# First batch element with all of V in fp32, low parts of the second over ScalarE and GpSimd, and a new program order for both

## The chip, the cores and the metric

The kernel runs on one core of one Trainium2 chip. The metric is device time in microseconds (us) of one execution. The engines are TensorE (PE, its weight loads PEld), VectorE (DVE), ScalarE (ACT), GpSimd (POOL) and SyncE (SP, which here only issues DMAs). Each runs its own instructions strictly in the order in which the program lists them and waits on semaphores for the others.

## The reference, cut to what matters

```python
# x: (8, 8, 512, 64), state: (8, 8, 32, 64)
xread = softmax(x @ state.T / 8) @ state        # 512 tokens per batch element and head
sread = softmax(state @ x.T / 8) @ x            # 32 slots per batch element and head
x = concat([xread, sread], axis=2)              # -> 8*544 tokens, 512 features
h = x @ w_in                                    # w_in: 512 x 2048
g = where(h >= 1, h, where(h <= -1, 0, (h + 1)**2 / 4))
x = g @ w_out                                   # w_out: 2048 x 512
...
logits = x @ phi                                # soft MoE: 32 slots, softmax over tokens and over slots
out = c @ (relu(slot_input @ w1) @ w2)          # 8 experts
```

## The kernel before, in words

The 8 batch elements are called b = 0 to 7; a ninth pass (b = 8) takes the state tokens. For one b, `attention(b)` makes the attention weights a (two halves G, each 128 x 512), and `vchunk(b, c)` multiplies the state with a quarter c of `w_in`, which gives V (two halves of 128 x 512 in PSUM). `hstep(b, m)`, m = 0 to 15, then makes a block h of 128 x 512 of the hidden layer as V times a, since xread @ w_in = a @ (state @ w_in); chunk c serves m = 4c to 4c+3.

fp32 products are made exact enough in one of two ways. In the *split* form each operand is written as a high part in fp32r (ACT copies it) and a low part in fp32r (the operand less its high part, a subtraction), and h is the sum of six fp32r matmuls: per half G high by high, high by low and low by high (line 478). In the *plain* form h is the sum of two fp32 matmuls (line 469). Before, only chunk 0 of b = 0 is plain. Every other chunk of V has two low parts, made by DVE at line 428 (`v<-V,v`), or, for the entries of the table `lP` and 2 <= b < 7, by an extra ACT copy `Vs` and a GpSimd subtraction (line 426).

The activation takes h to g: ACT makes c = relu(h/2 + 1/2) out of PSUM, GpSimd squares it (line 508), DVE makes g = min(max(h, 1), c) (line 532). Three PSUM banks hold h (`psH`), so the h of m + 3 needs the g of m. DVE then transposes g into `gp` (line 552, `tstep`); four transposes belong to four m. `estep` multiplies four g with the product of w_out and phi, `smblock(b)` updates the running softmax and `fall` accumulates.

`w_in` and `w_out` come as 64 bit numbers. They are loaded in 16 pieces of 1 MB into six staging buffers, and `words(i, ...)` turns piece i into fp32: ACT copies two bytes per number into a rim (two instructions, 128x1024 bytes each), and DVE makes two passes (lines 169 and 171). For the pieces in `dv`, DVE makes three passes alone (lines 156, 158, 160). Pieces 0 to 7 are `w_in` (chunk c needs 2c and 2c+1), 8 to 15 are `w_out`; of the latter each pair is multiplied with phi (`wps`) and written back to DRAM. The conversions of pieces 2 to 15 lie between the hsteps of b = 0, as do the steps of `attention(1)`.

From b = 2 on, `steady` sets an order on PE that is written by hand and repeats for each b. For b = 0 and b = 1 the main loop sets it (`V0`, `Vn`: at which m a chunk's V is made; `E0`, `T0`: estep and transposes of b = 0; `attA`: steps of attention(2) in b = 1), and a scheduler orders each engine's list from that program order and the dependencies.

PSUM for V (`psV`) is one tile of two banks. The attention scores S of b = 1 and 2 lie in the same tile.

Of the kernel before, what the change touches and what calls it, by code (L numbers as in the profile page):

```python
# [17 lines left out]


@with_exitstack  # L20
def kernel(
# [14 lines left out]
    nc = tc.nc  # L36
# [180 lines left out]
    def attention(b):  # L217
# [180 lines left out]
    v0t = []

    def vlate(b):  # L400
        if not v0t:
            v0t.append(slot("v0", dt=F32R))
        return hilo(v0t[0])
# [473 lines left out]
    A = None  # L877
    for b in range(B + 1):
        last = b == B
        if 2 <= b < B:  # L880
# [9 lines left out]
            run["s_gc"] = slot("s_gc", tag="v1")  # L890
        for m in range(NM):
            if b == 0:
                for _ in range(CFG["todo"][m]):
                    todo.pop(0)()
            if last and m == 0:
                give("a1")
# [42 lines left out]
            if b == 1:
# [187 lines left out]
```

## Time and profile before

| | |
|---|---|
| Time, median of 3 runs | 508.49 us (507.92 to 510.24) |
| The profiled execution | 508.4 us |
| Its span, first to last instruction | 506.6 us |
| PE, DVE, ACT, POOL busy | 89%, 73%, 53%, 46% of the span |
| Mean granted clock of TensorE | 0.958 of full speed |

The span has three stages: loads, conversions and b = 0 (to about 93 us), b = 1 to 7 (41.7 us for each in the steady part), and the ninth pass with the experts. An average over the span says little on the first stage, so the rows further down are taken stretch by stretch.

### The profile page before, as it was taken

The page shows a single profiled execution, that of the slowest core. Times are in us where ns is not written, and L with a number is a line of the kernel's source. Part 1 is how long each engine was busy: PE and PEld are TensorE (multiplying, and loading weights), DVE is VectorE, ACT ScalarE, POOL GpSimd, SP SyncE. Part 2 cuts the span into 40 slices and gives each one's busy share as a digit, 9 for nine tenths or more (in the row PEclk, how much of TensorE's full clock was granted, in tenths as well). Part 3 has the DMA queues.
Part 4 walks back from the last instruction along what each step waited for, and adds up shares of the span by engine and source line. Part 5 has one row for each costly group of instructions (what it writes and reads, how often), then busy time and mean ns, then how long its engine had stood idle before and what let it go on. Part 6 is the DMA issues. An engine that isn't in the chain of part 4 may idle for free.

```text
span 506.6 us, 11018 instructions
## 1 busy us (share of the span) xinstructions
PE 451.7 (89%) x4497; PEld 262.5 (52%) x4497; DVE 371.1 (73%) x670; ACT 269.9 (53%) x485; POOL 234.6 (46%) x224
## 2 busy tenths in 40 slices
PE   5397859989999999999999999999989999897881
PEld 3133424545555565546555565556647798533450
DVE  2878997997797797699779779778788785340341
ACT  2899667463673674476367367455445476210331
POOL 2344533563873785586488379465442100020320
PEclk9679978999999999999999999999999999997995
DMA  8999756600310220220040031033054597799699
GB/s 311 419 421 416 232 208 216 242 1 3 96 72 1 84 85 1 84 85 0 3 167 2 2 98 71 1 98 153 2 208 144 193 403 292 286 425 413 238 307 293
DMA packets 22689, 85.83 MB, mean 169 GB/s; under 512 B 2032, under 2 KB 10608, under 8 KB 14576
## 3 DMA queue, kind: packets, MB, share of 16 engines
q1 hardware_dynamic: 22128, 84.62, 44.8%
q8 instruction: 35, 0.57, 0.5%
q0 software_dynamic: 512, 0.53, 0.5%
q14 instruction: 14, 0.11, 0.1%
HBM read 72.03 MB, written 13.11 MB: 168 GB/s over the span
## 4 chain that ended last, share of the span: by engine, by line
PE 51%; DVE 26%; DMA 10%; ACT 5%; POOL 3%; issue 2%; SPq 0%; DVEq 0%; ACTq 0%; POOLq 0%
PE h L478 19%; DMA w<-in_w_dram 6%; DVE gp L552 5%; DVE g L532 5%; PE h L486 4%; PE E L118 4%; PE FV L124 3%; PE V L118 3%; DMA gp<-in_win_dram 3%; PE FX L124 2%; PE SO L1034 2%; DVE wD L171 2%; DVE z L281 2%; PE wtp L783 2%; POOL a L316 2%
## 5 line engine op out<-in xcount | busy, mean ns | idle before, releaser
L478 PE MATMUL h<-a,v 128*128 128x512 f32 x744 | 198.4, 410 | 10.8 <-DVE g L532 5.2
L508 POOL TENSOR_TENSOR c<-c 128x512 f32<-128x512 f32 x128 | 136.2, 1071 | 127.1 <-ACT c L129 117.9
L478 PEld LDWEIGHTS h<-a,v 128*128 128x128 f32 x744 | 133.2, 190 | 83.9 <-issue 29.5
L129 ACT ACTIVATE c<-h,half 128x512 f32<-128x512 f32 x128 | 87.9, 690 | 102.6 <-PE h L478 79.9
L532 DVE SCALAR_TENSOR_TENSOR g<-h,c 128x512 f32<-128x512 f32 x112 | 75.7, 676 | 20.9 <-POOL c L508 20.7
L552 DVE STREAM_TRANSPOSE gp<-g 128x512 f32<-128x512 f32 x112 | 78.9, 705 | 2.3
L129 ACT ACTIVATE v<-V 128x512 fp32r<-128x512 f32 x62 | 37.4, 603 | 12.7 <-PE V L124 7.8
L118 PE MATMUL V<-win,st_t 64*32 64x512 f32 x64 | 34.4, 618 | 2.8 <-ACT att L129 2.8
L124 PE MATMUL V<-win,st_t 64*32 64x512 f32 x448 | 36.7, 618 | 0.0
L124 PE MATMUL FX<-gp,dR 32*32 32x512 f32 x512 | 35.6, 598 | 0.0
L124 PE MATMUL FV<-gp,dR 32*32 32x512 f32 x496 | 35.4, 597 | 0.0
L118 PE MATMUL E<-g,wp 128*32 128x512 f32 x56 | 29.2, 604 | 1.8 <-DVE g L532 1.4
L428 DVE TENSOR_TENSOR v<-V,v 128x512 fp32r<-128x512 f32 x42 | 28.3, 674 | 2.7 <-ACT v L129 2.2
L124 PE MATMUL E<-g,wp 128*32 128x512 f32 x168 | 29.6, 605 | 0.0
L284 POOL TENSOR_TENSOR att<-att,z 128x512 f32<-128x512 f32 x16 | 18.1, 1136 | 24.1 <-DVE rz L246 16.8
L426 POOL TENSOR_TENSOR v<-Vs,v 128x512 fp32r<-128x512 f32 x20 | 25.9, 1294 | 5.1 <-ACT Vs L129 5.1
L486 PE MATMUL h<-XSh,v 128*128 128x256 f32 x128 | 25.0, 287 | 0.0
L661 DVE SCALAR_TENSOR_TENSOR acc<-acc,al,FV 128x256 f32<-128x256 f32 (+1 forms) x20 | 10.6, 584 | 18.1 <-PE FX L124 18.1
L1069 DVE COPY o<-oV 128x512 f32<-128x512 f32 x6 | 4.2, 692 | 25.6 <-PE oX L124 25.6
L1077 POOL DMA_DIRECT2D out_dram<-o x16 | 8.0, 509 | 30.4 <-DVE o L1069 30.4
L486 PEld LDWEIGHTS h<-XSh,v 128*128 128x128 f32 x128 | 20.2, 188 | 1.2 <-issue 0.8
L271 PE MATMUL eTp<-cst_t,att 128*128 128x128 f32 x64 | 11.3, 305 | 10.2 <-ACT att L129 10.1
(242 smaller groups left out, 779.5 us busy)
## 6 DMA issues: line engine op xcount, KB each, us to landing
w<-in_w_dram SPq DMA_DIRECT2D x22, 1024.0 KB, 9.6
xn<-in_xn_dram SPq DMA_DIRECT2D x8, 1024.0 KB, 4.9
out_dram<-o SPq DMA_DIRECT2D x16, 512.0 KB, 5.5
xs<-in_xs_dram SPq DMA_DIRECT2D x7, 1024.0 KB, 4.8
gp<-in_w_dram SPq DMA_DIRECT2D x6, 1024.0 KB, 7.6
gp<-in_wout_dram SPq DMA_DIRECT2D x5, 1024.0 KB, 10.4
wb<-in_win_dram SPq DMA_DIRECT2D x4, 1024.0 KB, 12.3
wo<-wD SPq DMA_DIRECT2D x16, 256.0 KB, 3.3
```

What stands on the lines that cost most here:

```text
L118: first = mm(**calls[0])
L124: e = mm(**c)
L129: return nc.scalar.activation(out=out, in_=in_, func=func, **kw)
L271: nc.tensor.transpose(p[:, st, :], e2[G][:, 128 * st:128 * st + 128], ident)
L284: (nc.vector if b in CFG["mulD"] else nc.gpsimd).tensor_tensor(out=t3, in0=t3, in1=z1.unsqueeze(2).to_broadcast([128, 16, 32]), op=ALU.mult)
L426: nc.gpsimd.tensor_tensor(out=lo[:, G, :], in0=Vs, in1=hi[:, G, :], op=ALU.subtract)
L428: nc.vector.tensor_tensor(out=lo[:, G, :], in0=V[G], in1=hi[:, G, :], op=ALU.subtract)
L478: mm(out=h, lhsT=v[:, G, f], rhs=a[:, G, :], start=(k == 0), stop=(k == 5))
L486: mm(out=h, lhsT=w[:, j, :], rhs=x[:, j, :], start=(k == 0), stop=(k == 11))
L508: nc.gpsimd.tensor_tensor(out=c, in0=c, in1=c, op=ALU.mult)
L532: gI[b, m] = nc.vector.scalar_tensor_tensor(out=g, in0=h, scalar=1.0, in1=c, op0=ALU.max, op1=ALU.min)
L552: nc.vector.transpose(out=gd_of(b, m), in_=gT[b, m])
```

## The change

Four edits to code and a set of tables:

- `f32` lists the chunks of b = 0 that are plain: now 0, 1, 2 and 3. Their V goes out of PSUM in two ACT copies, with no low parts; a of b = 0 is used as it is, so its high parts (two ACT copies) and low parts (two GpSimd subtractions, line 316) are gone. All 16 hsteps of b = 0 are two fp32 matmuls.
- `lP1` sends six of the eight low parts of b = 1 over the ACT copy `Vs` and GpSimd: all but (chunk 0, G 0) and (chunk 3, G 1). (`lP0` has no effect, since no chunk of b = 0 is split.)
- `gv0` and `gv1` let ACT square c, instead of GpSimd, for m = 3, 5, 11 of b = 0 and m = 4, 6 of b = 1.
- Order: chunks 1, 2, 3 of b = 0 at m = 2, 4, 6 (were 2, 6, 10) and of b = 1 at m = 1, 4, 8 (were 0, 4, 10); the conversions at other m (`cpos`); pieces 7 and 9 on DVE alone (were 10 and 12); the steps of attention(1) and attention(2), the esteps and transposes of b = 0 at other m; 10 warming matmuls instead of 14.

```diff
-CFG = dict(..., dv=(10,12), V0=(2, 6, 10), Vn=(0, 4, 10), ..., warm=14, ...)
+CFG = {'cpos': (1, 1, 2, 4, 4, 5, 8, 9, 10, 11, 11, 11, 12, 13), ..., 'lP1': ((0, 1), (1, 0), (1, 1), (2, 0), (2, 1), (3, 0)), ..., 'f32': (0, 1, 2, 3), ...}
...
         def back():
+            araw[b] = raw
+            if b == 0 and 3 in CFG["f32"]:
+                for G in range(2):
+                    nc.vector.transpose(out=raw[G], in_=T1[G])
+                return
...
-        if (b, c) == (0, 0) and CFG["f32c"]:
-            vf = slot("vf", tag="v0").rearrange("p (w g f) -> p w g f", w=2, g=2)[:, 0]
+        if b == 0 and c in CFG["f32"]:
+            vf = vtile(c // 3, F32)[c % 2]
             Vt[b, c] = (vf, vf)
...
-            if (c, G) in CFG["lP"] and 2 <= b < 7:
+            if (c, G) in (CFG["lP0"] if b == 0 else CFG["lP1"] if b == 1 else CFG["lP"] if b < 7 else ()):
                 Vs = rot_q.tile([128, 512], F32, tag="q", name="Vs")
...
-        if (b, c) == (0, 0) and CFG["f32c"]:
+        if b == 0 and c in CFG["f32"]:
             for G in range(2):
-                mm(out=h, lhsT=Vt[0, 0][0][:, G, 128 * mm_:128 * mm_ + 128], rhs=araw[0][G], start=(G == 0), stop=(G == 1))
+                mm(out=h, lhsT=Vt[0, c][0][:, G, 128 * mm_:128 * mm_ + 128], rhs=araw[0][G], start=(G == 0), stop=(G == 1))
...
-        v = (CFG["gv0"] if b == 0 else CFG["gvS"] if b == B else CFG["gv"])[m]
+        v = (CFG["gv0"] if b == 0 else CFG["gvS"] if b == B else CFG["gv1"] if b == 1 else CFG["gv"])[m]
...
-                for _ in range(CFG["todo"][m]):
+                for _ in range(CFG["cpos"].count(m)):
                     todo.pop(0)()
```

From the middle of b = 2 on, every engine's list is the same in both kernels. Three places of the lists:

On DVE, in the middle of b = 0 (`win` and `wD` are pieces of the weights being converted, `gp<-h,c` is g, `v_113<-V` a low part of V). Before:

```order
L428 TENSOR_TENSOR v_113<-V,v_113 128x512
L169 TENSOR_SCALAR win_107<-wb_112 128x1024
L428 TENSOR_TENSOR v_113<-V,v_113 128x512
L532 SCALAR_TENSOR_TENSOR gp<-h,c 128x512
L171 SCALAR_TENSOR_TENSOR win_107<-gp,win_107 128x1024
L169 TENSOR_SCALAR wD<-ast 128x1024
L532 SCALAR_TENSOR_TENSOR gp<-h,c 128x512
L171 SCALAR_TENSOR_TENSOR wD<-LT,wD 128x1024
```

Now:

```order
L155 TENSOR_SCALAR win_107<-wb_112 128x1024
L157 SCALAR_TENSOR_TENSOR win_107<-wb_112,win_107 128x1024
L537 SCALAR_TENSOR_TENSOR gp<-h,c 128x512
L159 SCALAR_TENSOR_TENSOR win_107<-wb_112,win_107 128x1024
L168 TENSOR_SCALAR wD<-ast 128x1024
L537 SCALAR_TENSOR_TENSOR gp<-h,c 128x512
L170 SCALAR_TENSOR_TENSOR wD<-LT,wD 128x1024
```

The two low parts between the conversions are gone, and piece 7 is converted by three DVE passes without ACT.

On PE, around the last chunk of b = 0 (`V<-win_107` is chunk 3, `V<-win_104` chunk 0 of b = 1; `h<-a_115,v_113` split, `h<-spare,v_383` plain, both from chunk 3). Before:

```order
L271 MATMUL eTp<-cst_t,att 128x128 x4
L118 MATMUL wps<-wD,phi_t 32x512
L124 MATMUL wps<-wD,phi_t 32x512 x3
L118 MATMUL V<-win_107,st_t 32x512
L124 MATMUL V<-win_107,st_t 32x512 x7
L198 MATMUL wps<-cst_t,wsb 128x32 x4
L118 MATMUL wps<-wD,phi_t 32x512
L124 MATMUL wps<-wD,phi_t 32x512 x3
L478 MATMUL h<-a_115,v_113 128x512 x6
```

Now:

```order
L117 MATMUL V<-win_107,st_t 32x512
L123 MATMUL V<-win_107,st_t 32x512 x7
L270 MATMUL eTp<-cst_t,att 128x128 x4
L117 MATMUL wps<-wD,phi_t 32x512
L123 MATMUL wps<-wD,phi_t 32x512 x3
L474 MATMUL h<-spare,v_383 128x512 x3
L117 MATMUL V<-win_104,st_t 32x512
L123 MATMUL V<-win_104,st_t 32x512 x7
L474 MATMUL h<-spare,v_383 128x512
L197 MATMUL wps<-cst_t,wsb 128x32 x4
```

Chunk 3 stands ahead of the second group of transposes of attention(1) and of two `wps`, and the first hsteps from it stand before three of the `wps` groups instead of after.

On POOL, at the end of b = 1 (`v_..<-Vs` is a low part of V, `a_..<-att` a low part of a, `c<-c` a square). Before:

```order
L508 TENSOR_TENSOR c<-c 128x512 x4
L316 TENSOR_TENSOR a_115<-att,a_115 128x512
L508 TENSOR_TENSOR c<-c 128x512
L316 TENSOR_TENSOR a_115<-att,a_115 128x512
L426 TENSOR_TENSOR v_382<-Vs,v_382 128x512
L508 TENSOR_TENSOR c<-c 128x512
L426 TENSOR_TENSOR v_382<-Vs,v_382 128x512
```

Now:

```order
L513 TENSOR_TENSOR c<-c 128x512 x2
L431 TENSOR_TENSOR v_725<-Vs,v_725 128x512
L431 TENSOR_TENSOR v_608<-Vs,v_608 128x512
L513 TENSOR_TENSOR c<-c 128x512
L431 TENSOR_TENSOR v_608<-Vs,v_608 128x512
L321 TENSOR_TENSOR a_114<-att,a_114 128x512
L513 TENSOR_TENSOR c<-c 128x512
L321 TENSOR_TENSOR a_114<-att,a_114 128x512
```

One more low part (`v_725`, chunk 3 of b = 1) stands in this stretch, and the low parts of chunk 0 of b = 2 (`v_382`, now `v_608`) have moved ahead of those of a.

## Rows read from the trace of the kernel before

**Rows 1.** Stretches: length, busy us (x instructions) by engine, granted clock, DMA share, GB/s
```profile
21.93:97.35 75.42, 61.44 (x454) 30.44 (x450) 65.87 (x90) 55.83 (x80) 34.18 (x27) 0.87 0.79 297
50.00:60.00 10.00, 8.45 (x57) 4.23 (x56) 10.00 (x12) 6.35 (x9) 3.59 (x3) 1.00 0.65 227
93.05:137.41 44.36, 42.44 (x421) 23.35 (x421) 36.55 (x73) 24.07 (x47) 25.20 (x24) 1.00 0.17 63
179.20:220.90 41.70, 40.69 (x423) 23.23 (x422) 34.83 (x64) 24.41 (x47) 28.09 (x27) 1.00 0.15 50
```

**Rows 2.** Chain that ended last, 59 to 65 us: start, duration, what
```profile
59.00 1.12 DVE wD L171
...
61.98 2.40 DVE gp L552 x4
```

**Rows 3.** DVE groups by form, 21.93 to 97.35: count | busy, mean ns | idle before
```profile
L552 DVE STREAM_TRANSPOSE gp<-gp 128x512 f32<-128x512 f32 x12 | 7.4, 675 | 0.0
L428 DVE TENSOR_TENSOR v<-V,v 128x512 fp32r<-128x512 f32 x10 | 6.8, 682 | 2.3 <-ACT v L129 2.2
```

**Rows 4.** What DVE waited for, 21.93 to 97.35: total us, times, longest
```profile
DVE v L428 <- ACT v L129: 2.2, 3, 0.9
DVE win L171 <- ACT LT L129: 1.8, 2, 1.5
```

**Rows 5.** Timeline of all engines, 23 to 28 us: start, duration, instruction [idle before]
```profile
23.38 3.48 POOL L316 TENSOR_TENSOR a<-spare,a 128x512 fp32r<-128x512 f32 x2 [0.48 <-ACT a L129]
23.57 2.16 DVE L171 SCALAR_TENSOR_TENSOR win<-LT,win 128x1024 uint32<-128x1024 uint32 x1
25.65 2.36 DVE L169 TENSOR_SCALAR win<-gp 128x1024 uint32<-128x1024 uint32 x2
```

**Rows 6.** Timeline, PE: plain and split hsteps (x counts records, two for one fp32 matmul)
```profile
24.85 8.33 PE L469 MATMUL h<-spare,vf 128*128 128x512 f32 x12 [1.78 <-ACT vf L129]
36.13 1.98 PE L469 MATMUL h<-spare,vf 128*128 128x512 f32 x4
98.05 3.02 PE L478 MATMUL h<-a,v 128*128 128x512 f32 x12
```

**Rows 7.** PE, stretches of 2 us: length, busy (x instructions), granted clock, DMA share, GB/s
```profile
28.00:30.00 2.00, 2.00 (x3) 0.50 1.00 418
62.00:64.00 2.00, 2.00 (x6) 0.50 0.89 330
70.00:72.00 2.00, 2.00 (x24) 0.57 0.00 0
72.00:74.00 2.00, 1.56 (x24) 1.00 0.00 0
76.00:78.00 2.00, 2.00 (x10) 0.50 0.74 262
```

**Rows 8.** Timeline, 66 to 97 us: the last chunk of b = 0, the last rim, the first g of b = 1
```profile
71.29 0.80 PE L118 MATMUL V<-win,st_t 64*32 64x512 f32 x1
75.99 0.57 ACT L129 ACTIVATE v<-V 128x512 fp32r<-128x512 f32 x1
77.31 0.60 ACT L129 ACTIVATE v<-V 128x512 fp32r<-128x512 f32 x1 [0.59 <-DVE v L428]
78.29 2.58 ACT L129 ACTIVATE LT<-gp 128x1024 uint8<-128x1024 uint8 x2
96.66 0.69 DVE L532 SCALAR_TENSOR_TENSOR g<-h,c 128x512 f32<-128x512 f32 x1 [0.52 <-POOL c L508]
```

**Rows 9.** POOL groups by form, 93.05 to 137.41 (b = 1)
```profile
L508 POOL TENSOR_TENSOR c<-c 128x512 f32<-128x512 f32 x15 | 15.6, 1040 | 19.3 <-ACT c L129 19.3
L426 POOL TENSOR_TENSOR v<-Vs,v 128x512 fp32r<-128x512 f32 x2 | 2.6, 1280 | 0.0
```

**Rows 10.** What PE waited for in b = 1, 93 to 137.4
```profile
PE h L478 <- DVE rz L246: 1.3, 1, 1.3
PE h L478 <- DVE gp L532: 0.6, 1, 0.6
```

More of the change, by code (lines that the diff above doesn't have):

```diff
@@ new lines @@
+CFG = {'cpos': (1, 1, 2, 4, 4, 5, 8, 9, 10, 11, 11, 11, 12, 13), 'at0': (4, 6, 7, 10, 11, 11, 12, 13, 13, 15), 'lP0': ((0, 0), (0, 1), (2, 0), (3, 0), (3, 1)), 'lP1': ((0, 1), (1, 0), (1, 1), (2, 0), (2, 1), (3, 0)), 'gv1': 'EEEESESEEEEEEEEE', 'f32': (0, 1, 2, 3), 'wsm': 13, 'xsP': 0, 'eng': ('PE',), 'wt8': (7, 8, 9, 10, 11, 12, 13, 14), 'wte': 'AD', 'wb': 12, 'gv6': (5, 9, 12), 'lP': ((0, 0), (0, 1), (1, 0), (3, 0)), 'attA': (7, 7, 8, 8, 9, 10, 12, 12), 'attB': (0, 1, 10, 11, 12), 'attN': (14, 15), 'dv': (7, 9), 'fl': -0.484375, 'hp': 2000, 'att7': (3, 5, 6, 7, 8, 10), 'og': 1, 'n3': 1, 'n3m': 10, 'wS': ['DP', 'AD', 'AD', 'AD', 'AD', 'DP', 'AD', 'DD', 'AD', 'AD', 'AD', 'AD', 'AD', 'AD', 'AD', 'AD'], 'xsm': 13, 'k0': 5, 'rg': 6, 'spg': 0, 'att0': 6, 'att': 7, 'V0': (2, 4, 6), 'Vn': (1, 4, 8), 'Vx': 12, 'wn': 'H', 'wsev': 'adad', 'conv': (4, 8, 9, 11, 12, 13, 19, 21, 24, 26, 28, 32, 36, 40, 44, 48, 52, 56, 60), 'todo': [1, 1, 1, 2, 0, 0, 0, 3, 0, 0, 2, 2, 1, 1, 0, 0], 'E0': ((0, 10), (0, 12), (0, 15), (1, 0)), 'T0': ((0, 13), (0, 15), (1, 0), (1, 1)), 'sm0': 5, 'E': 1, 'sm': 1, 'tqB': (5, 9, 13), 'GP': 0, 'pe': (3,), 'psH': 3, 'gtpX': (0, 7), 'tq0': (13, 15), 'keep': (2, 3, 4, 5), 'x2': (1, 2), 'natm': 1, 'warm': 10, 'bounce7': (0, 3), 'split': 1, 'wt': 4, 'so': 'cscscscscssss', 'smm': (1, 2, 3, 4, 5, 6, 9), 'tqv': (), 'tqvm': 0, 'first': 'x', 'apath': 2, 'f32c': 1, 'place': 1, 'attm': (3, 6, 7, 8, 9, 12), 'subPm': True, 'loDm': False, 'bounce': (0, 1, 2, 3), 'bq': ('s', 's'), 'xq': 's', 'nat': ((1, 11), (2, 2), (2, 3), (2, 11), (3, 2), (3, 4), (3, 9), (4, 2), (4, 3), (4, 9), (5, 2), (5, 3), (5, 9), (6, 2), (6, 4), (6, 9)), 'subP': (1,), 'mulD': (), 'loD': (), 'qlag': 0, 'gv0': 'EEESESEEEEESEEEE', 'gv': 'EEEEEEEEEEEEEEEE', 'gvS': 'BBBBBBBBBBBBBBBB'}
@@ L89 @@
     wb_s = [slot(f"wb{c}") for c in range(NW)]
-    v_s = [slot(f"v{c}", dt=F32R) if c or not CFG["f32c"] else None for c in range(2)]
     a_st = slot("ast", tag="a1")
@@ L307, in back @@
             aT[b] = (hi, lo)
-            araw[b] = raw
             for G in range(2):
@@ L313, in rest @@
         def rest():
+            if b not in aT:
+                return
             hi, lo = aT[b]
@@ L397, with vtile @@
     Vt = {}
[L398 to L403, printed above, removed]
+    vlate = {}
+    def vtile(i, dt):
+        if (i, dt) not in vlate:
+            vlate[i, dt] = slot(f"v{i}", dt=dt)
+        return hilo(vlate[i, dt])
     def vchunk(b, c):
@@ L417, in vchunk @@
             return
-        hi, lo = hilo(v_s[c % 2]) if not CFG["f32c"] or c % 2 else vlate(b)
+        hi, lo = vtile(c % 2, F32R)
         Vt[b, c] = (hi, lo)
@@ L453, in wsplit @@
         w = win_t[c][:, :, 128 * mm_:128 * mm_ + 128]
-        h, l = [v0t[0][:, 1024 * (m % 2) + 512 * i:1024 * (m % 2) + 512 * i + 512].rearrange("p (j f) -> p j f", j=4) for i in range(2)]
+        h, l = [vlate[0, F32R][:, 1024 * (m % 2) + 512 * i:1024 * (m % 2) + 512 * i + 512].rearrange("p (j f) -> p j f", j=4) for i in range(2)]
         x, y = CFG["wS"][m]
@@ L879 @@
         last = b == B
+        if b == CFG.get("stop"):
+            return
         if 2 <= b < B:
@@ L929 @@
             if not last:
+                if vg is not None and (m in (CFG["V0"] if b == 0 else CFG["Vn"]) or m == CFG["Vx"]):
+                    drain(vg)
                 if m in (CFG["V0"] if b == 0 else CFG["Vn"]):
@@ L947 @@
                     step(nx)
-            elif A is not None and (m >= CFG["att0"] if b == 0 else m in (CFG["att7"] or CFG["attm"] if b == B - 2 else CFG["attm"])):
-                if not step(A):
-                    A = None
+            elif A is not None and b == 0:
+                for _ in range(CFG["at0"].count(m)):
+                    step(A)
             if last and m in CFG["wt8"]:
```

1 line of the change is left out of this document (removed).

## The prediction

> **What bounds the kernel now.** I read the busy time by stretches first [rows 1], because the change touches only b = 0 and b = 1; after the middle of b = 2 the lists of all engines are the same. A steady b takes 41.70 us and PE is busy in 40.69 of it, so nothing there leaves room. b = 1 takes 44.36 with PE busy in 42.44: also PE, with 1.9 to spare. The stretch before it is another matter. From 21.93 (first transpose of a) to 97.35 (end of the first g of b = 1: 96.66 + 0.69 [rows 8]) there are 75.42 us, in which DVE is busy for 65.87, PE for 61.44, ACT for 55.83 and POOL for 34.18 [rows 1]. Between 50 and 60 DVE is busy in 10.00 of 10.00. Second I read the chain that ended last [rows 2]: it runs through DVE's conversions and transposes there. So in b = 0 DVE is the limit, with 9.55 us of waits (75.42 less 65.87), some on ACT [rows 4]; in b = 1 PE is.
>
> **The change part by part.** The sum is made for the profiled execution, 508.4 us (span 506.6 and 1.8 around it); the median of the runs is 508.49, so the two may be taken as one.
>
> *Low parts leave DVE.* Ten of the x10 low parts of rows 3 lie in the stretch: six of b = 0, four of b = 1 (chunks 0 and 1). Now one is left (chunk 0, G 0). Nine at 0.682 [rows 3] are 6.1 us off the engine that sets the end. In the rest of b = 1 three more go (2.0 us), but PE is the limit there, so I count them at nothing.
>
> *Transposes move in.* The list of DVE has four groups of four transposes ahead of the first g of b = 1 where there were three (x12 in rows 3). Four at 0.62 (7.4 for 12) put 2.5 us into the stretch. They leave b = 1, where DVE has room.
>
> *Waits of DVE.* Of the 9.55 us, 2.2 stand ahead of low parts, which ACT's copies hold up [rows 4]; both go with them. To see what comes in their place I laid the two new lists of DVE and ACT next to each other by hand, each operation at the duration that it has in the trace and not before its operands. ACT loses the two copies of a (1.3 us) and gains three squares and two to three copies Vs, some 3.5; with 19.6 us free in the stretch it can carry that. ACT's last rim ends near 75 to 78, against 80.9 before (78.29 + 2.58 [rows 8]), since chunk 3 no longer stands between the rims. The waits that I find (rims of pieces 3 to 6, squares by POOL, V of chunk 0 of b = 1 coming out of PSUM) add up to 6 to 7. I take 6.5, so 3 us go; between 0 and 5.
>
> *DVE and POOL in each other's way.* While POOL makes the two low parts of a (3.48 for two, against 1.28 for one such operation in b = 1 [rows 9]), a DVE pass takes 2.16 [rows 5], against 1.12 in the chain [rows 2], and the two after it 2.36 where two of 0.7 would do. These two POOL operations go, some 2 us, and three squares go to ACT, up to 0.9 more. The first of it lies ahead of ACT's rims, which come no earlier, so of 2.9 I take 1, between 0 and 2.9. The Trainium skill, "SBUF — State Buffer", section "Who interferes with whom", says that a DVE instruction with two SBUF inputs and a GpSimd instruction that reads SBUF exclude each other for their whole length. By it the six new POOL low parts of b = 1 could stop DVE as well, which speaks against the change; but of DVE's work in b = 1 only the last conversions have two SBUF inputs, and the sum by that page would be 1 to 2 us worse, 502 to 503.
>
> *Plain instead of split.* Twelve hsteps of b = 0 change form. A split one takes 3.02 / 12 x 6 = 1.5, with the last end in it; steady 1.43 (a start every 0.239). A plain one at full clock takes four records of 0.43, so 1.71 (four in 1.98 with the last end [rows 6]). PE gets 12 x 0.28 = 3.3 us more. At the low clock (0.50, which is 1.2 GHz [rows 7]) a record takes 0.85, so a plain hstep takes 3.41: twelve records lasted 8.33, most of them at the low clock [rows 6]. PE has 14 us of waits in the stretch, and it runs behind DVE and ACT, so most is covered; I put 1 us on the path, between 0 and 3.4 (two hsteps of chunk 3 at the low clock, as at 62 to 64 and 76 to 78, after PE's waits [rows 7]). The Trainium skill, "FP8 and Floating Point Precision", section "TensorE Precision Notes", counts a true fp32 product as four passes. By that a plain hstep would be eight passes against six, a third more, where the rows say a fifth; 12 x 2 passes of 0.24 would be 5.8 on PE instead of 3.3, and if none of the difference were covered the time would be 503.5.
>
> *b = 1 itself.* PE waits there 1.9 us for DVE [rows 10]: scores and their small operations stood ahead of a g. With DVE relieved of three low parts and four transposes, I take 0.8 of that as gained, between 1.9 and a loss: see the second rival. POOL gets six low parts of 1.28 (7.7 us), loses two squares of 1.04, and waits 19.3 us for c [rows 9], so on the average it has room. The reads of the second PSUM tile, the DMA queue and the fewer warming matmuls (PE waits for ACT right after them in both) I put at nothing: the weights' pieces land before DVE or ACT come to them, and pieces 14 and 15 are asked for earlier.
>
> The sum: -6.1 + 2.5 - 3 - 1 + 1 = -6.6 in the stretch, -0.8 in b = 1; -7.4 in all, and 508.4 - 7.4 = 501.0. Everything later moves with it, since the weights of the experts are loaded into buffers that b = 6 and later set free.
>
> **The rivals.** *The freed time turns into new waits (506.4).* V of chunk 3 lies in the PSUM that holds the scores of b = 1, so it cannot be made before both exponentials are out. That was so before (V at 71.29, copies at 75.99 and 77.31 [rows 8]) and it still is. If ACT's order keeps the copy near 72 or later, DVE's waits stay at 9.55 and four plain hsteps run at the low clock, 1.71 more each, half of it covered (3.4 instead of my 1): -6.1 + 2.5 - 1 + 3.4 - 0.8 = -2.0. Against it: ACT's list has that copy ahead of three rims' worth of work which stood before it.
>
> *POOL becomes the bound at the end of b = 1 (504.8).* Between the last hsteps POOL now makes three low parts of V, two of a and three squares: 5 x 1.28 + 3 x 1.04 = 9.5 us, while PE has four hsteps there (5.7). If that gap stands on the path, 3.8 come back. For it: the g needs the square, and the h needs the g three blocks earlier. Against it: PE also has V, scores and transposes in that place, and before there were two low parts of V, two of a there too, with a wait of PE of only some tenths.
>
> *Slower: the plain hsteps meet a cold PE (512).* A plain block at the low clock costs 1.71 more than at the full one. If PE waits so often that m = 8 to 15 all run there, that is 13.7, on top of 2.2 for their form; PE's waits take some 5 of it, and 501.0 + 15.9 - 5 gives 512. It decides from the sixth such block on: (7.4 + 2.5) / 1.71 = 5.8. In the trace the clock was low around 62 to 64, 70 and 76 to 78, with full clock between [rows 7]; of the new list two blocks or so would fall into such a time.
>
> *More than the sum (497).* If PE picks up b = 1 as soon as a is ready and no longer trails DVE by three blocks, b = 1 starts 8 to 9 us earlier, and its waits go: -11.
>
> **How the numbers follow.** Forecast 501.0 with chance 0.60; new waits 506.4 with 0.10; POOL 504.8 with 0.12; cold PE 512 with 0.08; more than the sum 497 with 0.10. The forecast's own bounds are -6.1 + 2.5 - 5 - 2.9 - 1.9 = -13.4 at best and -6.1 + 2.5 + 3.4 = -0.2 at worst if all ends met at once; half of that to either side is likely. The range goes from 496.5 to 506.0: it holds the forecast, the POOL case and most of the gain above, and leaves out the cold PE (0.08), about half of the new waits and the far end of the gain. Half a per cent, 2.5 us, is about what a measurement of this kernel can tell from none. Faster by more: 0.60 + 0.12 + 0.10 = 0.82. The same: 0.10. Slower: 0.08.
>
> **What would show it.** In the profile after, the first g of b = 1 should end near 91, DVE should be busy for about 59 to 61 us from 22 to there, and b = 2 should begin near 130 instead of 137.41, with steady b of 41.7 as before. The copy of V chunk 3 should come at 65 to 70. The low parts on DVE should be two in b = 0 and 1 together. If b = 1 takes over 46 us with PE waiting for g and g for POOL, the second rival holds; if the granted clock is at 0.50 for most of 45 to 80, the third. If b = 2 starts later than 135, the forecast is wrong in b = 0, and the size of DVE's waits there is the step to look at.

## The result, and the profile after

| | before | after |
|---|---|---|
| Time, median | 508.53 us (507.92 to 510.24) | 495.11 us (494.73 to 496.84) |
| Ratio | | 0.9747, 95% interval 0.9715 to 0.9778 |
| Profiled execution, its span | 508.4, 506.6 | 496.84, 495.1 |
| End of the first g of b = 1, 2, 3 | 97.35, 144.45, 187.16 | 88.52, 132.29, 174.73 |

13.4 us faster, where 7.4 were forecast; 495.1 lies below the range. The profiled execution of after took 1.7 us more than the median; its mean granted clock is 0.972, where another execution has 0.98. Where two kernels are compared by stretches below, the mark is the end of a first g. From the mark of b = 3 to the end all kernels of this document do the same work, and their profiled executions took between 318 and 323 us for it, so the mark tells small differences better than the total does.

The stretches of the kernel after: the first, b = 1, a steady b, then 28 us to the first g of b = 3, and 60 to 80. Columns as in [rows 1].

```profile
21.76:88.52 66.76, 61.14 (x448) 25.46 (x440) 58.18 (x86) 56.80 (x85) 29.82 (x25) 0.96 0.87 336
78.73:124.69 45.96, 44.24 (x450) 24.36 (x446) 37.08 (x74) 27.55 (x56) 31.34 (x28) 1.00 0.31 104
124.69:166.40 41.71, 40.01 (x419) 23.13 (x420) 34.91 (x66) 23.82 (x45) 27.58 (x27) 1.00 0.18 58
28.00:174.73 146.73, 138.94 (x1274) 70.38 (x1272) 125.64 (x223) 104.20 (x183) 87.88 (x78) 1.00 0.46 171
60.00:80.00 20.00, 18.55 (x179) 7.90 (x163) 17.20 (x29) 16.69 (x28) 7.54 (x8) 1.00 0.63 227
```

The same two last stretches of the kernel before (its mark is at 187.16).

```profile
28.00:187.16 159.16, 143.70 (x1299) 76.69 (x1297) 136.48 (x237) 102.29 (x174) 87.07 (x77) 0.96 0.43 158
60.00:80.00 20.00, 13.03 (x99) 6.61 (x103) 17.04 (x32) 13.94 (x21) 8.57 (x7) 0.74 0.58 204
```

The first stretch fell from 75.42 [rows 1] to 66.76, 8.7 us; from the first g of b = 1 to that of b = 2 it was 47.10 and is 43.77, another 3.3; a steady b is 41.7 as before. Over both together DVE's ledger shows where the time went: from 28 us to the first g of b = 3 the time fell by 12.43, DVE's busy time by 10.84 (136.48 to 125.64) and its idle time by only 1.6 (22.7 to 21.1). From 60 to 80 us PE worked at full clock throughout (1.00, before 0.74).

What DVE waited for in the first stretch of after, against [rows 4] (us in all, times, longest):

```profile
DVE gp L557 <- PE E L123: 1.9, 1, 1.9
DVE win L170 <- ACT LT L128: 1.6, 1, 1.6
DVE gp L537 <- POOL c L513: 1.6, 3, 0.9
DVE v L433 <- ACT v L128: 1.6, 1, 1.6
```

The waits are others, but hardly fewer: 8.58 (66.76 less 58.18) against 9.55. So little of the gain is in waits; DVE has less to do: nine low parts are gone, and its conversions take less. First the one-input pass of line 169 in the first stretch of before: ns min/median/max, first and last start.

```profile
L169 DVE TENSOR_SCALAR wD<-gp x4: 654/677/687, 49.8 to 81.5; 128x1024 uint32<-128x1024 uint32 x4
L169 DVE TENSOR_SCALAR win<-gp x3: 681/705/1762, 25.7 to 31.8; 128x1024 uint32<-128x1024 uint32 x3
L169 DVE TENSOR_SCALAR win<-wb x2: 715/1066/1416, 36.0 to 40.6; 128x1024 uint32<-128x1024 uint32 x2
L169 DVE TENSOR_SCALAR wD<-ast x1: 1533/1533/1533, 45.0 to 45.0; 128x1024 uint32<-128x1024 uint32 x1
L169 DVE TENSOR_SCALAR wD<-wb x1: 1543/1543/1543, 68.7 to 68.7; 128x1024 uint32<-128x1024 uint32 x1
```

The same line (now 168) in the first stretch of after.

```profile
L168 DVE TENSOR_SCALAR wD<-gp x4: 652/684/781, 48.2 to 73.7; 128x1024 uint32<-128x1024 uint32 x4
L168 DVE TENSOR_SCALAR win<-gp x3: 682/686/687, 24.5 to 29.8; 128x1024 uint32<-128x1024 uint32 x3
L168 DVE TENSOR_SCALAR win<-wb x1: 1414/1414/1414, 32.3 to 32.3; 128x1024 uint32<-128x1024 uint32 x1
L168 DVE TENSOR_SCALAR wD<-wb x2: 644/660/676, 62.6 to 63.2; 128x1024 uint32<-128x1024 uint32 x2
L168 DVE TENSOR_SCALAR wD<-ast x1: 681/681/681, 42.0 to 42.0; 128x1024 uint32<-128x1024 uint32 x1
```

One instruction, one shape, two prices: about 0.7, or 1.4 to 1.8. Four of the eleven passes have the higher price before, one after. The eleven take 10.89 together before and 8.03 after; all 29 passes of the conversions take 35.18 before and 29.88 after, 5.3 less.

### The profile page after: what moved, and what is told of

It is laid out like the page before. It is cut to its first block, busy times and chain, and to the rows that moved or that the text cites. A ratio compares the mean times of both kernels' runs of the same rounds, so it can differ in the third digit from the quotient of the medians.

```text
span 495.1 us, 10947 instructions
## 1 busy us (share of the span) xinstructions
PE 445.9 (90%) x4465; PEld 255.4 (52%) x4465; DVE 358.9 (73%) x658; ACT 272.6 (55%) x494; POOL 232.1 (47%) x223
## 4 chain that ended last, share of the span: by engine, by line
PE 51%; DVE 25%; DMA 8%; ACT 7%; POOL 5%; issue 3%; SPq 0%; DVEq 0%; ACTq 0%; POOLq 0%
PE h L483 17%; DMA w<-in_w_dram 6%; DVE g L537 6%; DVE gp L557 5%; PE h L491 4%; PE E L117 4%; PE FV L123 3%; PE V L117 3%; PE h L474 2%; PE FX L123 2%; POOL a L321 2%; POOL c L513 2%; PE SO L1043 2%; ACT LT L128 2%; DVE mx L240 2%
## 5 line engine op out<-in xcount | busy, mean ns | idle before, releaser
L513 POOL TENSOR_TENSOR c<-c 128x512 f32<-128x512 f32 x123 | 130.1, 1063 | 108.4 <-ACT c L128 95.1
L483 PE MATMUL h<-a,v 128*128 128x512 f32 x672 | 175.5, 405 | 5.7 <-DVE g L537 4.4
L483 PEld LDWEIGHTS h<-a,v 128*128 128x128 f32 x672 | 119.8, 188 | 68.0 <-issue 25.3
L128 ACT ACTIVATE v<-V 128x512 fp32r<-128x512 f32 (+1 forms) x64 | 38.2, 605 | 11.6 <-PE V L123 9.3
L431 POOL TENSOR_TENSOR v<-Vs,v 128x512 fp32r<-128x512 f32 x26 | 33.6, 1293 | 11.1 <-ACT Vs L128 11.0
L474 PE MATMUL h<-spare,v 128*128 128x512 f32 x64 | 32.3, 640 | 5.2 <-ACT v L128 2.3
L117 PE MATMUL V<-win,st_t 64*32 64x512 f32 x64 | 34.2, 615 | 2.8 <-ACT att L128 2.8
L474 PEld LDWEIGHTS h<-spare,v 128*128 128x128 f32 x64 | 11.8, 200 | 24.5 <-issue 11.8
L433 DVE TENSOR_TENSOR v<-V,v 128x512 fp32r<-128x512 f32 x30 | 20.1, 670 | 1.9 <-ACT v L128 1.6
```

Source lines behind the costliest of these rows:

```text
L117: first = mm(**calls[0])
L128: return nc.scalar.activation(out=out, in_=in_, func=func, **kw)
L474: mm(out=h, lhsT=Vt[0, c][0][:, G, 128 * mm_:128 * mm_ + 128], rhs=araw[0][G], start=(G == 0), stop=(G == 1))
L483: mm(out=h, lhsT=v[:, G, f], rhs=a[:, G, :], start=(k == 0), stop=(k == 5))
L513: nc.gpsimd.tensor_tensor(out=c, in0=c, in1=c, op=ALU.mult)
```

## The experiments

The table gives for each kernel the median and the ratio to before with its interval, then, from its profiled execution, the stretch from 28 us to the end of the first g of b = 3, DVE's busy and idle time in it, and the time of the 29 conversion passes. "Low parts" are those of b = 1 on GpSimd, "squares" the five on ScalarE.

| kernel | median us | ratio, 95% | 28 to b = 3 | DVE busy | DVE idle | conversions |
|---|---|---|---|---|---|---|
| before | 508.5 | | 159.2 | 136.5 | 22.7 | 35.2 |
| plain form alone (e1) | 513.7 | 1.0109, 1.0046 to 1.0172 | 163.2 | 130.0 | 33.2 | 33.1 |
| order alone, lP0 at work (e2) | 514.1 | 1.0117, 1.0053 to 1.0181 | 163.2 | 139.7 | 23.5 | 38.5 |
| plain form, V early, conversions (p2) | 506.0 | 0.9979, 0.9946 to 1.0012 | 156.2 | 132.8 | 23.4 | 33.5 |
| squares alone (x3) | 511.0 | 1.0040, 1.0013 to 1.0066 | 160.6 | 133.5 | 27.1 | 34.3 |
| order alone (e2b) | 504.2 | 0.9917, 0.9886 to 0.9947 | 156.4 | 135.4 | 21.1 | 34.2 |
| order, low parts (x4) | 505.6 | 0.9939, 0.9911 to 0.9966 | 154.0 | 131.5 | 22.4 | 34.1 |
| all but the plain form (f0) | 501.9 | 0.9882, 0.9844 to 0.9919 | 153.1 | 130.3 | 22.8 | 31.9 |
| plain form, order (x1) | 500.5 | 0.9858, 0.9808 to 0.9909 | 151.3 | 132.0 | 19.4 | 33.9 |
| all but the squares (e4) | 500.1 | 0.9860, 0.9827 to 0.9893 | 150.2 | 129.2 | 21.0 | 33.9 |
| all but the low parts (e3) | 497.4 | 0.9811, 0.9755 to 0.9867 | 148.7 | 127.8 | 20.8 | 29.8 |
| after with the parts of a (e8) | 498.2 | 0.9822, 0.9785 to 0.9859 | 148.9 | 127.0 | 22.0 | 31.9 |
| after, V at 2, 6, 10 (v1) | 508.6 | 1.0007, 0.9978 to 1.0036 | 158.5 | 126.6 | 31.9 | 30.4 |
| after | 495.1 | 0.9747, 0.9715 to 0.9778 | 146.7 | 125.6 | 21.1 | 29.9 |
| after, three low parts (h1) | 494.1 | 0.9742, 0.9712 to 0.9771 | 145.8 | 128.2 | 17.6 | 30.4 |
| the same, two squares more (h5) | 494.0 | 0.9739, 0.9699 to 0.9779 | 145.1 | 126.6 | 18.5 | 28.7 |

In all but three rows DVE idles for 17.6 to 23.5 us, and the time roughly goes with DVE's busy time. The three others (e1, x3, v1) idle for 27 to 33: there the work saved came back as waiting.

One caution holds for most rows. The scheduler orders the lists anew for every edit, so that a row holds some change of order beside the part that it is named for. Only two pairs keep the lists of DVE and PE as they are (compared in the traces up to the first g of b = 3): e8 against after, and h5 against h1.

**The two halves apart.** Plain form with the old tables, and the new tables without the plain form:

```diff
 # e1: old cpos, at0, attA, dv, V0, Vn, E0, T0, sm0, warm, x2
-'lP1': ((0, 1), ...), 'gv0': 'EEESES...', 'gv1': 'EEEESES...'
+'lP1': (), 'gv0': 'EEEEEE...', 'gv1': 'EEEEEEE...'
 # e2: new tables
-'f32': (0, 1, 2, 3), 'lP1': ((0, 1), ...), gv0, gv1 as above
+'f32': (0,), 'lP1': (), gv0, gv1 all E
```

> Only the plain form: all four chunks of b = 0 in fp32, all tables of order as before, low parts of b = 1 and all squares as before. Theory A (the work that leaves VectorE and GpSimd in b = 0 carries the gain): six low parts off VectorE, 6 x 0.68 = 4.1, two low parts of a off GpSimd, which stretch VectorE's passes, 2 to 4; chunk 3 of V still late, so a plain block or two at 0.50 of the clock: 501 to 503. Theory B (the new order carries the gain: V of chunk 3 earlier, TensorE not behind VectorE when b = 1 begins): 506 to 508, or above 508 if the plain blocks meet the low clock.

> Only the new order: chunks 1 to 3 of b = 0 split again with two low parts on VectorE each, a of b = 0 with its high and low parts, no low part of b = 1 on GpSimd, no square on ScalarE; tables of order as in the changed kernel. Theory A: the ten low parts stand on VectorE again ahead of the end of the first stretch, plus four transposes: 505 to 509. Theory B: 498 to 501.

Neither range of either run holds its time: 513.7 and 514.1, each slower than before. What DVE waited for in e1 up to the first g of b = 2:

```profile
DVE gp L537 <- POOL c L513: 6.1, 5, 3.0
DVE acc L664 <- PE FX L123: 6.0, 1, 6.0
DVE wD L170 <- ACT LT L128: 3.6, 2, 2.0
```

DVE's busy time did fall by 6.5 (136.5 to 130.0), as theory A wants, but 10.5 us of new waits came for it: for squares and rims in b = 0, and for PE in b = 1. The longest of the five waits for squares, 3.0 us, goes back to PE: ACT made the c of that square at 81.27, right after the end of two plain hsteps that ran mostly at the low clock:

```profile
75.44 5.79 PE L474 MATMUL h<-spare,v 128*128 128x512 f32 x8
```

In v1 below, eight such records at the full clock take 3.70. From 28 us to the first g of b = 1 the granted clock of e1 is 0.88, against 0.91 before and 1.00 after. So the last clause of theory B (plain blocks that meet the low clock) has a part in this run; how large a part is not shown. Its first g of b = 1 ends at 96.60, 0.75 earlier, that of b = 2 at 146.32, 1.9 later than before.

The run of the order alone was spoilt by a detail: `lP0`, which has no effect in the changed kernel, works again once chunks of b = 0 are split. So three low parts of b = 0 were on GpSimd in it, and in the run that was to be its base, contrary to what their expectations say. Without the new order (e0) that costs 0.5% by the medians (510.5, 1.0047, 1.0013 to 1.0082) and 0.1 us by the mark at b = 3 of its profiled execution (187.29):

> All four edits undone inside the changed program: old tables, only chunk 0 plain, all low parts of b = 1 on VectorE, no square on ScalarE. It is the base for the two runs that do one half each. Every theory: 508.5, within 1 us; if it is further off, the way in which the loop was rewritten (drains of the V steps) is itself part of the change.

With `lP0` empty the base has the order of before on all engines, so before itself is the base, and the order alone was run again:

```diff
-'f32': (0, 1, 2, 3), 'lP0': ((0, 0), ...), 'lP1': ((0, 1), ...), gv0, gv1 as above
+'f32': (0,), 'lP0': (), 'lP1': (), gv0, gv1 all E
```

> The order alone once more. In the runs of the base and of the order alone, three of the six low parts of b = 0 were on GpSimd, since the table lP0 works once a chunk of b = 0 is split; here all six are on VectorE, as before. If the order without the plain form loses by itself (theory C): 510 to 515. If the three low parts on GpSimd were the loss (theory B): 500 to 508.

504.2: the order alone is faster by 4, and the three low parts on GpSimd in b = 0 cost 9.9 by the medians (514.1 to 504.2), 6.8 by the mark at b = 3 (the profiled execution of e2b, 507.85, is its slowest). GpSimd's low parts in the first stretch of e2 (1.78 each, where [rows 9] have 1.28):

```profile
L431 POOL TENSOR_TENSOR v<-Vs,v 128x512 fp32r<-128x512 f32 x3 | 5.3, 1779 | 0.9 <-ACT Vs L128 0.9
```

The conversions of that kernel take 38.5, those of e2b 34.2: taking three low parts from DVE (2.0 us) gave it 4.3 us more in other passes. Beside the conversions GpSimd is no free engine.

**What the plain form lacked alone.** e1 with three of the new tables:

```diff
-V0=(2, 6, 10), cpos of before, dv=(10, 12)
+V0=(2, 4, 6), cpos of after, dv=(7, 9)
```

> The kernel of the run with the plain form alone, with three of the new tables added: where the chunks of V of b = 0 are made (2, 4, 6), where the conversions stand, and which pieces VectorE converts alone. All other order as before. If what the plain form lacks is an early chunk 3 and the order of the conversions (theory A): the first stretch falls from 74.7 to 67 to 70, b = 1 stays at 47 to 50, so 504 to 508. If it needs the order of attention, E and transposes as well: within 2 us of the plain form alone, 511 to 514.

506.0, in theory A's range for the time, though the first stretch fell only to 72.2 (21.74 to 93.96). DVE's idle time went from 33.2 back to 23.4. Against before that is still no gain (the interval holds 1). The remaining tables of order (`Vn`, the steps of attention, E, transposes, warming and two small ones) are all that x1 below adds to this run. They are worth 5.5 together (506.0 to 500.5, intervals apart); no run takes them apart. And the converse, the changed kernel with only `V0` as before:

```diff
-'V0': (2, 4, 6)
+'V0': (2, 6, 10)
```

> The changed kernel, with the chunks of V of b = 0 made at m = 2, 6, 10 as before instead of 2, 4, 6. Theory A (the plain form pays only with an early chunk 3, since otherwise VectorE's freed time becomes waits): copies of chunk 3 at 70 or later instead of 62.6, the first stretch 4 to 8 longer, 499 to 503. Rival (the order of the conversions alone does it): 495 to 497.

508.6, worse than both: one table takes the whole gain. My theory named the wrong chunk. Chunk 3 is copied at 65.92, 3.3 later than in after; it is chunk 2 that hangs. PE in v1, 39 to 56 us (start, duration, [idle before]):

```profile
39.17 0.61 PE L117 MATMUL S<-xs,st_t 64*32 64x512 f32 x1
...
44.63 1.98 PE L474 MATMUL h<-spare,v 128*128 128x512 f32 x4 [0.74 <-DVE gp L537]
53.78 1.06 PE L117 MATMUL V<-win,st_t 64*32 64x512 f32 x1 [7.16 <-ACT att L128]
```

PE in after, 39 to 46 us:

```profile
39.09 0.61 PE L117 MATMUL V<-win,st_t 64*32 64x512 f32 x1
...
40.10 5.42 PE L474 MATMUL h<-spare,v 128*128 128x512 f32 x12
45.45 0.61 PE L117 MATMUL S<-xs,st_t 64*32 64x512 f32 x1
```

S of b = 1 and V share one PSUM tile. The new order starts attention(1) early; with chunk 2 behind S, PE waits 7.16 for the exponentials, and V then takes 1.06 for a matmul instead of 0.61, since the clock fell during the wait. `V0` and the steps of attention belong together.

**One part out of the changed kernel at a time.** No plain form but in chunk 0 (f0); all low parts of b = 1 on DVE (e3); all squares on GpSimd (e4):

```diff
 # f0
-'f32': (0, 1, 2, 3), 'lP0': ((0, 0), ...)
+'f32': (0,), 'lP0': ()
 # e3
-'lP1': ((0, 1), (1, 0), (1, 1), (2, 0), (2, 1), (3, 0))
+'lP1': ()
 # e4
-'gv0': 'EEESESEEEEESEEEE', 'gv1': 'EEEESESEEEEEEEEE'
+'gv0': 'EEEEEEEEEEEEEEEE', 'gv1': 'EEEEEEEEEEEEEEEE'
```

> The changed kernel, with chunks 1 to 3 of b = 0 split again (their six low parts on VectorE, as before) and a of b = 0 with its high and low parts; all else as changed. If the plain form's worth is its own work (theory A): 6 x 0.68 = 4.1 on VectorE, 2.1 for the parts of a (measured by themselves), less what TensorE gains (0.28 x 12 = 3.3, at most half of it on the path): 500 to 502. If the parts of the change need each other (theory C): as the order alone did, 5 to 10 more, 505 to 510.

> The changed kernel with all eight low parts of b = 1 on VectorE. Three of those six lie ahead of the first g of b = 1 (3 x 0.68 = 2.0 there), three in b = 1, where TensorE is the limit. Theory A: 497 (2 us back), b = 1 itself as long as in the changed kernel within 0.5. Theory B: 495 to 496, since TensorE no longer trails VectorE. If the low parts were a loss on GpSimd (they stretch VectorE's passes): 493 to 494.

> The changed kernel, with all squares of c on GpSimd (five more, 1.06 each). Theory A: three of them lie in the first stretch, where VectorE waits for them or its passes are stretched, 0.3 to 0.7 each, and two in b = 1: 496 to 497. Rival: the squares are covered, within 0.5 of the changed kernel's 495.1.

f0: 501.9, as theory A had it, so in the new order the plain form is worth 6.8 (6.3 by the mark at b = 3). e3: 497.4, theory A's number, but by another way; its interval and that of after overlap, and at the mark of b = 3 it is 1.9 later. Its first stretch and b = 1 (to the first g of b = 2):

```profile
22.20:86.44 64.24, 59.45 (x432) 25.54 (x424) 57.56 (x84) 55.12 (x81) 26.11 (x22) 0.95 0.89 344
86.44:134.31 47.87, 42.88 (x439) 23.29 (x431) 40.20 (x84) 27.65 (x54) 26.11 (x26) 1.00 0.20 72
```

The first stretch is 2.5 shorter than in after and b = 1 4.1 longer. Most of the 2.5 is no gain, since four transposes of b = 0 stand behind the first g of b = 1 here. In the first stretch of after, then of e3 (count, busy us, mean ns, idle before):

```profile
L557 DVE STREAM_TRANSPOSE gp<-gp 128x512 f32<-128x512 f32 x16 | 9.9, 672 | 1.9 <-PE E L123 1.9
L557 DVE STREAM_TRANSPOSE gp<-gp 128x512 f32<-128x512 f32 x12 | 7.4, 670 | 0.0
```

So the 4.1 is the price of these transposes (2.5 of DVE's time) and of three low parts (2.0) together, in a stretch where I had priced both at nothing; h1 below takes them apart. e4: 500.1, five squares are worth 5 (3.5 by the mark at b = 3), not 1 to 2. DVE and GpSimd in e4, 37 to 43 us:

```profile
37.94 1.04 POOL L513 TENSOR_TENSOR c<-c 128x512 f32<-128x512 f32 x1 [0.59 <-ACT c L128]
38.00 1.53 DVE L155 TENSOR_SCALAR win<-wb 128x1024 uint32<-128x1024 uint32 x1
39.57 1.23 DVE L157 SCALAR_TENSOR_TENSOR win<-wb,win 128x1024 uint32<-128x1024 uint32 x1
39.99 1.70 POOL L513 TENSOR_TENSOR c<-c 128x512 f32<-128x512 f32 x1 [1.01 <-ACT c L128]
40.83 1.95 DVE L159 SCALAR_TENSOR_TENSOR win<-wb,win 128x1024 uint32<-128x1024 uint32 x1
```

The same place in after, where the square of m = 3 is on ScalarE:

```profile
37.97 0.68 DVE L155 TENSOR_SCALAR win<-wb 128x1024 uint32<-128x1024 uint32 x1
38.69 1.23 DVE L157 SCALAR_TENSOR_TENSOR win<-wb,win 128x1024 uint32<-128x1024 uint32 x1
```

A square on GpSimd that begins 0.06 us ahead of the pass makes 1.53 of 0.68: the pass ends 0.55 after the square's end (38.98), as if it had to let the square go first. The next square begins at 39.99, within the pass of line 157, and takes 1.70: it ends 0.89 after that pass (40.80), and the pass that follows takes 1.95. In the conversions e4 has 4.0 us more (33.9 against 29.9), and its first g of b = 1 comes 3.6 later.

**The parts of a by themselves.** The changed kernel makes the high and low parts of the first a again, which nothing reads:

```diff
 if b == 0 and 3 in CFG["f32"]:
     for G in range(2):
         nc.vector.transpose(out=raw[G], in_=T1[G])
+        act(hi[:, G, :], raw[G])
...
+    for G in range(2):
+        nc.gpsimd.tensor_tensor(out=lo[:, G, :], in0=raw[G], in1=hi[:, G, :], op=ALU.subtract)
```

> The changed kernel, with the high and low parts of the first a made as before (two copies on ScalarE, 1.3 us, two subtractions on GpSimd), though nothing reads them. Theory A (GpSimd's low parts stretch VectorE's conversions): the first pass of line 170 takes about 2.2 instead of 1.18, the conversions of the stretch add up to 32 to 34 instead of 30.0, and the first stretch ends 2 to 4 later: 497 to 499. Rival (it lies ahead of ScalarE's copies of the rims, and is covered): at most 1 later, 495 to 496.

498.2, and 2.1 later than after at the first g of b = 1 (90.65): theory A. The first two conversion rows, which are [rows 5] again:

```profile
23.69 2.15 DVE L170 SCALAR_TENSOR_TENSOR win<-LT,win 128x1024 uint32<-128x1024 uint32 x1
25.77 2.36 DVE L168 TENSOR_SCALAR win<-gp 128x1024 uint32<-128x1024 uint32 x2
```

The conversions are 2.0 longer, and all of it reaches the end of the stretch. DVE's and PE's lists are those of after, so here nothing but the added operations is at work.

**Do the parts add up.** Plain form and order only (x1); squares alone in the kernel before (x3); order and low parts, no plain form but in chunk 0 (x4):

```diff
 # x1, from after
+'lP1': (), gv0, gv1 all E
 # x3, from before
+gv0='EEESESEEEEESEEEE', gv1='EEEESESEEEEEEEEE'
 # x4, from after
+'f32': (0,), 'lP0': (), gv0, gv1 all E
```

> Plain form and new order, without the other two parts (all low parts of b = 1 on VectorE, all squares on GpSimd). Taken away one at a time from the changed kernel, the low parts were worth 2.3 and the squares 5.0. If the two add up: 495.1 + 7.3 = 502.4, between 501 and 504. If they pay for the same thing (GpSimd is relieved of one so that it can take the other): 497 to 500, since without the low parts GpSimd has room for the squares.

> The kernel before, with the squares of m = 3, 5, 11 of b = 0 and m = 4, 6 of b = 1 on ScalarE and nothing else. If a square that leaves GpSimd is worth what it frees in VectorE's conversions wherever it stands (0.9 for each that meets one): 504.5 to 507. If VectorE's freed time becomes waits in the old order, as it did for the plain form alone: 507.5 to 510.

> New order and the low parts of b = 1 on GpSimd; chunks 1 to 3 of b = 0 split, squares on GpSimd. Against the order alone (504.2) it adds the low parts; against the changed kernel without the plain form (501.9) it lacks the squares. If the low parts are worth their 2.3 here too: 501 to 503, and the squares nothing without the plain form. If the squares are worth 3 to 5 here too: 505 to 507, and the low parts lose without them.

x1: 500.5, between the two cases: together low parts and squares bring 5.4, singly 2.3 and 5.0 (by the mark at b = 3, 4.6 against 1.9 and 3.5). The runs of x1 spread from 500.0 to 504.1, so it is not shown that they pay in part for the same. x3: 511.0, above both of its ranges; squares alone gain nothing. They also free little there: its conversions take 34.3, 0.8 less than before, where the same squares are worth 4.0 in the new order. Its first stretch is 4.6 shorter (70.84), 1.4 of it by two low parts that the scheduler moved behind the first g, b = 1 is 5.2 longer (52.27), and what DVE waits for most up to the first g of b = 2 is again PE:

```profile
DVE acc L664 <- PE FX L123: 7.5, 1, 7.5
```

x4: 505.6 against 504.2 and 501.9. The median puts the gain on the squares, the mark at b = 3 (154.0, after 156.4 without the low parts; 153.1 with the squares too) on the low parts; the intervals of x4 and e2b overlap. This stays open.

**Further.** Two versions that follow from this. Only the last three low parts of b = 1 on GpSimd (h1), and with that two more squares on ScalarE (h5):

```diff
 # h1
-'lP1': ((0, 1), (1, 0), (1, 1), (2, 0), (2, 1), (3, 0))
+'lP1': ((2, 0), (2, 1), (3, 0))
 # h5, from h1
-'gv0': 'EEESESEEEEESEEEE'
+'gv0': 'SEESESESEEESEEEE'
```

> The changed kernel, with the low parts of chunks 0 and 1 of b = 1 on VectorE and only (2, 0), (2, 1), (3, 0) on GpSimd. With all of them on VectorE the first stretch was 2.5 us shorter than in the changed kernel (64.24 against 66.76) and b = 1 4.1 longer (47.87 against 43.77). If the loss in b = 1 comes from the low parts of chunks 2 and 3, this run has both: 492.5 to 494. If the two go together (transposes that move from the first stretch into b = 1), 495 to 497.

> The changed kernel, with the low parts of chunks 0 and 1 of b = 1 on VectorE and the squares of m = 0 and 7 of b = 0 on ScalarE as well, where a GpSimd square stretched a conversion pass of VectorE by 0.7 to 0.9 each. If VectorE's stretched passes set the end (theory A): 1 to 1.7 below the run without these two squares, 492.5 to 493.5. If ScalarE's queue does (two squares of 0.63 ahead of the rims): 494 to 495.5.

The first stretch and b = 1 of h1:

```profile
21.72:86.45 64.73, 59.77 (x432) 25.69 (x424) 58.11 (x84) 55.17 (x81) 25.68 (x22) 0.94 0.89 342
86.45:131.28 44.83, 42.65 (x440) 23.30 (x432) 39.05 (x82) 28.70 (x57) 30.23 (x29) 1.00 0.23 77
```

h1 has the transposes where e3 has them and differs from it in the low parts. Of the 4.1 that e3 lost in b = 1, three are back (47.87 to 44.83), so they come from the low parts of chunks 2 and 3; the last 1.1 goes with the transposes. 494.1, just above its first range, and 494.0, where the rival of h5 put it: both 1 us below after in the medians, and 1.0 and 1.6 earlier at b = 3, but the intervals of the ratios overlap with that of after. With the same lists on DVE and PE, the conversions of h5 take 1.7 less than those of h1 (28.7 against 30.4), as its theory A wanted; 0.65 of it arrives at the mark of b = 3, and 0.1 in the medians. So not every freed pass shortens the kernel.

## Why the prediction was wrong

*Low parts leave DVE*: nine at 0.68 left the stretch, as counted. *Transposes move in*: four more stand there (16 against 12), at the 2.5 taken.

*DVE and POOL in each other's way*: the step that failed most. I took 1 us of at most 2.9; the conversions fell by 5.3. Two errors. I looked closely at one place, two low parts of a beside two rows [rows 5], and gave three squares 0.9 in all, where the squares do the same all through the stretch: L169 had passes of 1.5 beside passes of 0.68 in the trace of before. Put back (e4), the squares cost 4.0 in the conversions. And I held that a gain ahead of the rims would be lost; e8 returns those 2 us in full. How the 5.3 divide depends on the rest: out of the changed kernel, parts of a and squares are worth 2.0 and 4.0 of conversions, in the old order 2.1 (e1, with the plain form) and 0.8 (x3). The Trainium skill, "SBUF — State Buffer", section "Who interferes with whom", of which I had used the sentence on two inputs, also names tensor_scalar among the operations that can take the pair of ports that VectorE and GpSimd share, for the whole instruction. The trace agrees: 0.68 alone, 1.53 behind a square of 1.04.

*b = 1 itself*: the second failure. I called PE the limit there because it is the busier engine, and put three low parts at nothing and the transposes' way out of b = 1 at nothing as well, after charging 2.5 for their way in. From first g to first g b = 1 lost 3.3 us. In e3, with low parts and transposes in b = 1 as before, it is 4.1 longer than in after; 3.0 of that are the low parts of chunks 2 and 3, and 1.1 is left for the transposes (h1). The forecast took 0.8, from the waits of PE alone [rows 10]. Over both stretches the transposes cancel, the low parts count (twelve at 0.68, 8.2) and the conversions (5.3): 13.5, near the 12.4 that the mark at b = 3 shows; DVE's busy time itself fell by 11.6 over the two stretches, 7.7 and 3.9.

*Waits of DVE*: 3 taken, 1.0 found. Of the 2.2 us ahead of low parts 1.6 are still there, for the one that is left, and 1.9 for PE's E are new; my list of 6 to 7 was too low. This error hid part of the other two: with 4.3 more from the conversions, 2.5 more from b = 1 and 2.0 less from the waits, 4.8 of the 6.0 us missed are told (5.0 by the mark at b = 3, which came 12.4 earlier).

*Plain instead of split, low clock*: +1 taken, about nothing found. By the mark at b = 3 the plain form is worth 6.3 (f0); six low parts at 0.68 (4.1) and the parts of a (2.2 by the same mark of e8) account for all of it. I moved the low clock of [rows 7] along with the chunks; in after it is 1.00 from 28 us to the first g of b = 3, and PE's waits of 14.0 us (75.42 less 61.44) became 5.6 (66.76 less 61.14). What the clock gave was not measured by itself.

*The rivals.* "More than the sum" (497, chance 0.10) is what happened, for the reason it gave in part: PE no longer trails. Its block m = 3 begins at 88.57, right after the first g of b = 1 (88.52); before, m = 2 began 0.7 after that g, at 98.05 [rows 6]. "New waits" is what the plain form does without the new order (e1, 513.7, worse than its 506.4). POOL as the bound did not come: PE waits 0.2 for g in b = 1, POOL is busy in 31.34 of 45.96. The cold PE did not come: the clock of the first stretch is 0.96. It shows in e1, where the plain form stands in the old order.

*The signs.* The first g of b = 1 ended at 88.52 for "near 91", DVE was busy for 58.18 in the stretch for "59 to 61", b = 2 began at 124.69 for "near 130", and the copy of chunk 3 came at 62.59 for "65 to 70": all past the forecast on the same side. The steady b and the two low parts came as said.

That the gain needs the order and the plain form together was not in the forecast. x1 gives 500.5, by chance about the number forecast for all of it.

## What to carry to other kernels

Price an instruction by its shortest record as well as its mean: where the same shape has two durations, something holds it up, and the difference times the count is work that can perhaps be taken away without removing the instruction. Where two engines exclude each other, moving work from one to the other can be a loss while the first has passes that the other stretches (three low parts in b = 0 in the new order, 9.9 us by the medians, 6.8 by the mark), and a gain where it has none (three low parts of b = 1, 3.0 us of that stretch). And sum what an engine saves over all stages up to the next fixed point rather than stage by stage, but ask first whether the order lets the others follow: the same saving was worth 6.8 us in one order and less than nothing in the other.

## What the runs showed of the hardware

A one-input pass of VectorE over 128x1024 took about 0.68 us alone and 1.53 where a GpSimd operation of 1.04 had begun just ahead of it; a two-input pass went from 1.2 to 1.95. It goes both ways: the GpSimd square took 1.70 where it met a pass under way, and low parts beside the conversions took 1.78 on average (e2) instead of 1.28 [rows 9].

PE's granted clock in v1 fell while it waited for 7.16 us, and the V matmuls after the wait took 1.06 against 0.61. This row of v1, of 2 us within the wait, shows it (0.50, no matmul):

```profile
50.00:52.00 2.00, 0.00 (x0) 0.00 (x0) 2.00 (x6) 2.00 (x4) 1.09 (x2) 0.50 1.01 415
```
